# One tile's operands made over three steps, its neighbour's results copied first and summed later, and sums of w_out moved away from the tile switches

## The chip, the cores and the metric

The kernel runs on one core of a Trainium2 chip. The metric is the device time of one execution in microseconds (us), measured on the chip; the profile is one such execution taken by the hardware profiler. The engines are named as in the profile: PE is the matmul engine (PEld its weight loads), DVE the vector engine, ACT the scalar engine, POOL the GpSimd engine, and SP the queue that issues all the DMAs here.

## The reference

The inputs are q, k and v for 8 batches, 8 heads, 576 tokens and 64 elements a head, a weight for the norm, and two weight matrices. Cut to what matters:

```python
kv = np.einsum('bhsd,bhse->bhde', k, v)
out = np.einsum('bhsd,bhde->bhse', q, kv)
rms = np.sqrt(np.mean(out * out, axis=-1, keepdims=True) + 1e-06)
attn = out / rms * g_norm
x = attn.transpose(0, 2, 1, 3).reshape(4608, 512)
h = x @ w_in                          # w_in is 512 x 2048
g = h * (1.0 / (1.0 + np.exp(-h)))
return g @ w_out                      # w_out is 2048 x 512
```

All in float32. The two large products are nearly all of the work.

## The kernel before

**Tiles and steps.** The 4608 tokens are nine tiles `t` of 512 (`TN`), and d_ff is 16 blocks of 128. float32 products are made of three matmuls each: every operand is split into an upper part (a rounded copy, made by ACT) and a lower part (what the rounding lost, a subtraction), and upper times upper, upper times lower and lower times upper are added up in PSUM.

Tiles 0 and 1 use plain products. From tile 2 the product with w_in is made with seven products of half-size blocks in place of eight (Strassen's scheme): `pair_step(t, i)` handles blocks `i` and `i + 8`, eight steps to a tile. Tiles 7 and 8 (`OUT7 = 7`) use seven products for w_out also: `seven_step(t, i)`. In it PE alternates between the w_in products of step `i` (`product(m, i, ...)`, 42 matmuls) and the w_out products of the step before it (`Half.multiply`, 42 matmuls, 21 for each `Half` of the tile's tokens) in four windows. So a seven-step is 84 matmuls of 128x128 by 128x256, and a pair step 90.

All code is written out in the order in which each engine executes it; there is no planner. `first_jobs`, `mid_jobs` and `last_jobs` hold work that is placed by hand at a third of a step `g = 16 t + 2 i` (a pair step or a seven-step spans `g` and `g + 1`).

**What the change touches.**

- The operands of the w_in products. `sums_of_x` makes four sums of the tile's quarters (x_sums, on DVE, 128x512), and `make_operand(m)` makes the upper part of operand `m` on ACT and the lower part on DVE or POOL. Each tile's operands overwrite those of the tile before, so `prepare` makes operand `m` in the last step (`i = 7`) of the tile before, right after the product that read the old one.
- The results of the w_out products. In PSUM each `Half` has seven sums in four banks: banks with (1, 2), (3, 5), (7, 6), and a bank with number 4 of both halves. `Half.results` adds them, from PSUM, to the two output chunks of the half: one copy on ACT and seven adds on DVE of 128x256, then two stores.
- The results of tile 6, the last of a plain w_out product: `project` copies a bank to SBUF after its last matmul, on ACT or DVE by turns, and stores it.
- `make_out_sums(j)`: the combinations of w_out that the last two tiles need, made on POOL over eight thirds of a step, split by ACT and DVE and stored to DRAM. One starts every eight steps from step 48, which is the beginning and the middle of tiles 3 to 6.
- `x_stages`: the scaling of the attention result to x32, a transpose and a multiply on DVE.
- The pool `tmp` has five places. The result copies (`ob`), the sums' tiles `s23` and `s41`, `x_sums`, `yT` and `sq` rotate through it, so that a tile can have to wait for the store of an earlier one.

Of the kernel before, what the change touches and what calls it, by code (L numbers as in the profile page):

```python
# [35 lines left out]
def linear_attention_rms_silu_ffn(  # L36
# [22 lines left out]
    nc = tc.nc  # L59
# [468 lines left out]

    def project(t, f, gh, gl, bank, n, cs):
# [7 lines left out]
        if f == last:  # L537
            ob = tmp.tile([P, S], F32, name="ob", tag="tmp")[:, :cs.stop - cs.start]
            (nc.scalar.copy if n % 2 else nc.vector.tensor_copy)(out=ob, in_=bank)
            nc.sync.dma_start(out=out[t * TN + n * P:t * TN + (n + 1) * P, cs], in_=ob)  # L540
# [8 lines left out]
    operands, x_sums, once = {}, {}, {}  # L549
# [130 lines left out]
    def make_operand(m, engine=nc.vector):  # L680
        j, x, _ = seven[m]
        upper, lower = operand(j)[:, 0], operand(j)[:, 1]
        nc.scalar.copy(out=upper, in_=x())
        engine.tensor_tensor(out=lower, in0=x(), in1=upper.bitcast(F32), op=ALU.subtract)

    def product(m, i, out, start=True, check=True):
        j, _, a_of = seven[m]
        x = operand(j)
        n = 0
        for c in range(2):  # L690
            for a, b in ((0, 1), (1, 0), (0, 0)):
                nc.tensor.matmul(  # L692
                    out=out, lhsT=a_of(i, a, c), rhs=x[:, b, c], start=start and n == 0, stop=n == 5,
# [88 lines left out]
    class Half:  # L782
# [57 lines left out]
        def banks(self, free, last):  # L840

            pairs = ((1, 2), (3, 5), (7, 6))
            self.out, self.opens = {}, {1, 3, 7}
            for (m, n), bank in zip(pairs, free):
                self.out[m], self.out[n] = bank[:, low], bank[:, high]
            self.out[4] = last[:, (low, high)[self.half]]
# [9 lines left out]
        def multiply(self, j, *ms):  # L856
            for m in ms:
                for n, (g, a) in enumerate(((self.hi, 1), (self.hi, 0), (self.lo, 0))):
                    nc.tensor.matmul(  # L859
                        out=self.out[m], lhsT=g[m], rhs=self.weight(m, j, a),  # L860
                        start=j == 0 and n == 0 and m in self.opens, stop=j == HF - 1 and n == 2,
                        skip_group_check=True,
                    )

        def results(self, t):
# [7 lines left out]
            def add(to, x, y, op=ALU.add):  # L873
                nc.vector.tensor_tensor(out=to, in0=x, in1=y, op=op)

            def store(tile_, chunk):
                row = t * TN + self.half * H + chunk * P
                nc.sync.dma_start(out=out[row:row + P, :], in_=tile_)

            return [  # L880
                lambda: nc.scalar.copy(out=p1, in_=out_of[1]),
                lambda: add(second[:, low], out_of[2], p1),
                lambda: add(u2, out_of[6], p1),
                lambda: add(u4, u2, out_of[5], ALU.subtract),
                lambda: add(first[:, low], out_of[3], u4),
                lambda: add(u3, out_of[7], u2),
                lambda: add(first[:, high], u3, out_of[5], ALU.subtract),
                lambda: store(first, 0),
                lambda: add(second[:, high], out_of[4], u3),
                lambda: store(second, 1),  # L890
            ]
# [18 lines left out]
    sevens = []  # L910

    def seven_step(t, i, groups):

        g = t * NF + 2 * i
        fresh, later = i == HF - 1 and t + 1 < NT, i + 1 < HF or t + 1 < NT
        if not sevens:
            once["products"], once["seventh"] = h_bank(), h_bank()
            once["forms"] = block("wi", HF + 5, F32).rearrange("p a n -> p a n")
            sevens.extend(Half(h) for h in range(2))
        before = (t, i) > (OUT7, 0)  # L920
        if (t, i) == (OUT7, 1):
            free = [ps_at.tile([P, 512], F32, name="at", tag=tag) for tag in ("at", "other")] + [once["seventh"]]
            last, *others = [acc_bank() for _ in range(4)]
            sevens[0].banks(free, last)
            sevens[1].banks(others, last)
        first, second = sevens
        j = (i - 1) % HF
        ends = before and i == 0
        scratch = place("scratch", 3, F32)
        p1, u2 = scratch[:, 1, 0], scratch[:, 1, 1]  # L930
# [3 lines left out]

        def old(n):
            for item in groups[:n]:
                project(*item)
            del groups[:n]

        def window(n):  # L940
            if groups:
                old(2)
            elif before:
                which = (first, second)[n // 2]
                which.multiply(j, *(which.order[:4], which.order[4:])[n % 2])
# [5 lines left out]
        def prepare(*ms):  # L951
            for n, m in enumerate(ms if fresh else ()):
# [422 lines left out]
```

## Time and profile before

| | us |
|---|---|
| median of 3 runs | 837.14 |
| lowest and highest | 833.77, 838.43 |
| the profiled execution, own time | 836.62 |
| its span in the trace | 834.7 |
| PE busy | 809.9 (97% of the span) |
| DVE busy | 586.6 (70%) |
| ACT busy | 385.4 (46%) |
| POOL busy | 200.9 (24%) |
| granted PE clock, mean over the span | 0.993 |

The profiled execution's time stands 0.5 us under the median and the span 1.9 us under its own time. A share of busy time is an average over the whole span; where PE is idle is read from its timeline.

### The profile page before, as it was taken

The page shows a single profiled execution, that of the slowest core. Times are in us where ns is not written, and L with a number is a line of the kernel's source. Part 1 is how long each engine was busy: PE and PEld are TensorE (multiplying, and loading weights), DVE is VectorE, ACT ScalarE, POOL GpSimd, SP SyncE. Part 2 cuts the span into 40 slices and gives each one's busy share as a digit, 9 for nine tenths or more (in the row PEclk, how much of TensorE's full clock was granted, in tenths as well). Part 3 has the DMA queues.
Part 4 walks back from the last instruction along what each step waited for, and adds up shares of the span by engine and source line. Part 5 has one row for each costly group of instructions (what it writes and reads, how often), then busy time and mean ns, then how long its engine had stood idle before and what let it go on. Part 6 is the DMA issues. An engine that isn't in the chain of part 4 may idle for free.

```text
span 834.7 us, 18341 instructions
## 1 busy us (share of the span) xinstructions
PE 809.9 (97%) x7388; PEld 800.1 (96%) x7388; DVE 586.6 (70%) x1184; ACT 385.4 (46%) x816; POOL 200.9 (24%) x193
## 2 busy tenths in 40 slices
PE   8999999999999999999999999999999999989996
PEld 7999999999999999999999999999999999888996
DVE  4999948786766666667866687577766667775666
ACT  4787545444542455335533463354434333442442
POOL 2798773331200043003120132004300000010000
PEclk9999999999999999999999999999999999999998
DMA  9993012356434453554527353745333576545552
GB/s 347 412 389 115 1 59 102 152 199 211 166 101 160 160 181 126 183 184 159 202 95 270 119 194 102 258 151 186 111 134 135 190 243 204 179 165 177 180 195 92
DMA packets 59670, 145.89 MB, mean 175 GB/s; under 512 B 5826, under 2 KB 20162, under 8 KB 59586
## 3 DMA queue, kind: packets, MB, share of 16 engines
q1 hardware_dynamic: 59586, 144.73, 50.3%
q8 instruction: 58, 0.95, 0.5%
q14 instruction: 26, 0.21, 0.1%
HBM read 118.49 MB, written 26.21 MB: 173 GB/s over the span
## 4 chain that ended last, share of the span: by engine, by line
PE 82%; DVE 7%; DMA 5%; ACT 2%; POOL 2%; issue 1%; SPq 1%; DVEq 0%; ACTq 0%; POOLq 0%
PE acc L494 32%; PE hp L692 29%; PE hp L494 9%; PE acc L859 4%; DMA wi<-in_moe_w_in 3%; PE at L859 2%; PE at L274 2%; PE hp L859 1%; DMA out<-ob 1%; DVE gl L706 1%; DMA k<-in_k 1%; PE at L307 1%; PE at L308 1%; PE at L309 1%; DVE x L335 1%
## 5 line engine op out<-in xcount | busy, mean ns | idle before, releaser
L494 PE MATMUL acc<-wo,gh 128*128 128x256 f32 x1792 | 279.5, 277 | 0.0
L494 PEld LDWEIGHTS acc<-wo,gh 128*128 128x128 f32 x1792 | 238.7, 188 | 0.4
L692 PE MATMUL hp<-x_second,wi 128*128 128x256 f32 x1344 | 172.5, 280 | 5.0 <-DVE gf L745 4.6
L494 PE MATMUL acc<-wo,gl 128*128 128x256 f32 x896 | 174.5, 276 | 0.0
L692 PEld LDWEIGHTS hp<-x_second,wi 128*128 128x128 f32 x1344 | 161.9, 189 | 7.2 <-DVE gf L745 5.4
L494 PEld LDWEIGHTS acc<-wo,gl 128*128 128x128 f32 x896 | 135.0, 188 | 0.0
L692 PE MATMUL hp<-operand,wi 128*128 128x256 f32 x1008 | 127.5, 278 | 3.3 <-DVE gated L1001 3.3
L692 PEld LDWEIGHTS hp<-operand,wi 128*128 128x128 f32 x1008 | 120.2, 188 | 4.6 <-DVE gated L1001 2.1
L295 POOL TENSOR_TENSOR ql<-q,qh 128x576 fp32r<-128x576 f32 x24 | 36.4, 1515 | 180.9 <-ACT qh L294 172.2
L596 POOL TENSOR_TENSOR s<-wo 128x512 f32<-128x512 f32 x16 | 23.8, 1500 | 156.9 <-DVE x L335 122.5
L744 ACT COPY wi<-hp 128x256 f32<-128x256 f32 x40 | 14.9, 372 | 89.0 <-PE hp L692 89.0
L702 ACT ACTIVATE gh<-gf 128x512 fp32r<-128x512 f32 x40 | 25.3, 633 | 56.5 <-DVE gf L757 52.2
L809 ACT ACTIVATE gated<-gated 128x512 f32<-128x512 f32 x32 | 20.3, 633 | 62.2 <-DVE gated L992 45.1
L494 PE MATMUL hp<-x_second,wi 128*128 128x256 f32 x384 | 46.3, 276 | 0.0
L494 PE MATMUL hp<-x,wi 128*128 128x256 f32 x360 | 44.7, 279 | 0.7 <-POOL x L445 0.7
L494 PEld LDWEIGHTS hp<-x_second,wi 128*128 128x128 f32 x384 | 44.9, 188 | 0.1
L494 PEld LDWEIGHTS hp<-x,wi 128*128 128x128 f32 x360 | 42.6, 188 | 1.2 <-POOL x L445 1.0
L702 ACT ACTIVATE gh<-wi 128x512 fp32r<-128x512 f32 x40 | 25.4, 635 | 38.7 <-DVE wi L757 34.7
L745 DVE TENSOR_TENSOR wi<-hp,wi 128x256 f32<-128x256 f32 x20 | 8.5, 424 | 46.2 <-ACT wi L744 46.2
L335 DVE SCALAR_TENSOR_TENSOR x<-o,gcol,yT 128x128 f32<-128x128 f32 (+7 forms) x52 | 37.9, 728 | 1.9
L745 DVE TENSOR_TENSOR gf<-hp,wi 128x256 f32<-128x256 f32 x20 | 8.5, 423 | 40.5 <-ACT wi L744 40.5
L313 ACT ACTIVATE sq<-at 128x256 f32<-128x256 f32 (+1 forms) x56 | 22.9, 409 | 28.9 <-PE at L309 28.2
(193 smaller groups left out, 1439.8 us busy)
## 6 DMA issues: line engine op xcount, KB each, us to landing
wi<-sums_in_dram SPq DMA_DIRECT2D x112, 512.0 KB, 3.4
s<-out_sums SPq DMA_DIRECT2D x48, 256.0 KB, 4.6
out<-ob SPq DMA_DIRECT2D x36, 256.0 KB, 2.3
wi<-in_moe_w_in SPq DMA_DIRECT2D x16, 512.0 KB, 8.0
wo<-in_moe_w_out SPq DMA_DIRECT2D x16, 512.0 KB, 9.0
sums_in_dram<-sum_parts SPq DMA_DIRECT2D x16, 512.0 KB, 2.6
out_sums<-wi SPq DMA_DIRECT2D x16, 512.0 KB, 2.9
k<-in_k SPq DMA_DIRECT2D x28, 288.0 KB, 5.1
```

Of the source, the lines that this page charges most:

```text
L274: nc.tensor.matmul(out=self.kv[h], lhsT=self.k[rows, c, :], rhs=self.v[rows, c, :], start=(start and r == 0), stop=(stop and r == 4),)
L295: (nc.vector if self.b == 1 else nc.gpsimd).tensor_tensor(out=self.ql, in0=self.q, in1=self.qh.bitcast(F32), op=ALU.subtract)
L313: nc.scalar.activation(out=self.sq[:, self.w], in_=self.ps, func=AF.Square)
L335: nc.vector.scalar_tensor_tensor(out=to, in0=self.o[:, a:e], scalar=gcol, in1=self.yT, op0=ALU.mult, op1=ALU.mult)
L494: nc.tensor.matmul(out=to[:, at:at + 256], lhsT=stationary, rhs=moving[:, at:at + 256], start=start and at == 0, stop=stop and at == n - 256,)
L596: nc.gpsimd.tensor_tensor(out=to, in0=w[:, 0, :], in1=w[:, 1, :], op=ALU.add)
L692: nc.tensor.matmul(out=out, lhsT=a_of(i, a, c), rhs=x[:, b, c], start=start and n == 0, stop=n == 5, skip_group_check=not check,)
L702: nc.scalar.activation(out=gh, in_=x, func=AF.Silu)
L744: nc.scalar.copy(out=p1, in_=u)
L745: nc.vector.tensor_tensor(out=c1[:, low], in0=v, in1=p1, op=ALU.add)
L809: nc.scalar.activation(out=self.gated, in_=self.gated, func=AF.Silu)
L859: nc.tensor.matmul(out=self.out[m], lhsT=g[m], rhs=self.weight(m, j, a), start=j == 0 and n == 0 and m in self.opens, stop=j == HF - 1 and ...
```

## The change

It has five parts.

1. The operands of tile 8 are no longer made in the last step of tile 7. A step has four places between the windows, called "", "I", "II" and "III", and a table `between` says what runs there. `spread_switch` places the four sums at steps 5 and 6 of tile 7 and the operands from step 6 to step 0 of tile 8. So that an operand can be made while the old one is still read, two operands go to free tiles, and the others each to the place of one that has been read already (`ahead`). All lower parts are made on DVE; none on POOL.
2. The results of tile 7 are copied from PSUM by ACT, four banks whole (128x512), and the adds then run on DVE out of SBUF, over steps 0 to 2 of tile 8 (`after_switch`).
3. The 42 w_out matmuls of a step are one queue, of which the windows take 12, 11, 11 and 8 (`W7`), in place of 12, 9, 12 and 9. After the last step the order of the products is another, and `last_results` does one subtraction per half on POOL and stores the second output chunk in two pieces.
4. The copies of tile 6's results are put off to step 1 of tile 7, all four on ACT (`emptied`).
5. `make_out_sums` starts four steps later each time, and the second `x_stages` of the last batch are at steps 1, 4, 6 and 8 after the tile's start in place of 1, 4, 7 and 10.

```diff
-            (nc.scalar.copy if n % 2 else nc.vector.tensor_copy)(out=ob, in_=bank)
...
+        if f == last and t + 1 == OUT7:
+            emptied.append(lambda: empty(t, bank, n, cs, True))
+        elif f == last:
+            empty(t, bank, n, cs, n % 2)
...
+    def make_upper(m, to):
+        nc.scalar.copy(out=to[0], in_=seven[m][1]())
+
+    def make_lower(m, to):
+        nc.vector.tensor_tensor(out=to[1], in0=seven[m][1](), in1=to[0].bitcast(F32), op=ALU.subtract)
...
+        def copies(self, places):
+
+            self.e = places
+            return [
+                lambda n=n, m=m: nc.scalar.copy(out=places[n], in_=self.bank_of[m]) for n, m in enumerate((1, 3, 7))
+            ]
...
+            return [
+                lambda: add(one[:, high], one[:, high], one[:, low]),
+                lambda: add(three[:, high], three[:, high], one[:, low]),
+                lambda: add(three[:, low], three[:, low], three[:, high]),
+                lambda: add(one[:, low], three[:, high], two[:, high], ALU.subtract),
+                lambda: add(two[:, high], three[:, low], two[:, high], ALU.subtract),
+                upper_rows, lower_rows,
+            ]
...
+            nc.scalar.copy(out=p5, in_=out_of[5])
+            add(u4, u2, p5, ALU.subtract, nc.gpsimd)
...
+    W7 = 12, 11, 11, 8
...
+        ahead.update({
+            1: spares, 6: [block6[:, 0], block6[:, 1]], 2: home(1), 7: home(6), 4: home(2), 5: home(7), 3: home(4),
+        })
+        x = sums_of_x()
+        between.update({
+            (5, "I"): x[:1], (5, "II"): x[1:3], (6, "I"): x[3:], (6, "II"): made_ahead(1, 6),
+            (7, "I"): made_ahead(2), (7, "II"): made_ahead(7, 4), (7, "III"): made_ahead(5),
+        })
...
+            (0, "I"): [c[0], *made_ahead(3)], (0, "II"): [c[1], c[2], a[0], a[1]], (0, "III"): a[2:4],
+            (1, ""): [lambda: nc.scalar.copy(out=fourths, in_=once["fourths"])],
+            (1, "I"): [d[0], d[1], *a[4:6]], (1, "II"): [d[2], a[6], b[0], b[1]], (1, "III"): b[2:4],
+            (2, "I"): b[4:6], (2, "II"): b[6:],
...
-        def prepare(*ms):
-            for n, m in enumerate(ms if fresh else ()):
-                make_operand(m, (nc.gpsimd, nc.vector)[n % 2])
...
-        first.multiply(HF - 1, *first.order)
-        run(first.results(t))
-        second.multiply(HF - 1, 1, 2, 6, 5, 3, 7, 4)
-        run(second.results(t))
+        for half, order in ((first, (1, 2, 6, 7, 5, 3, 4)), (second, (4, 1, 2, 6, 7, 5, 3))):
+            for item in half.items(HF - 1, order):
+                half.multiply(*item[1:])
+        for half in sevens:
+            half.last_results(t, once["partial"][:, half.half])
...
-            x_stages(p, b * NF + 1 + p.c * (3 if b >= OUT7 else 1), 1)
+            x_stages(p, b * NF + (1, 4, 6, 8)[p.c] if b >= OUT7 else b * NF + 1 + p.c, 1)
...
-            spread_out(lambda j=j: make_out_sums(j), 3 * (3 * NF + 8 * j), 1, 1, 1, 1, 1, 1, 1, 1)
+            spread_out(lambda j=j: make_out_sums(j), 3 * (3 * NF + 4 + 8 * j), 1, 1, 1, 1, 1, 1, 1, 1)
```

Where the instructions stand in the queues shows more than the diff. DVE, the end of step 6 of tile 7 and the first half of step 7, before: L1001 and L968 take the w_in products out of PSUM (`hp`), L830, L822 and L825 make the forms (`wi13`) of the gated values, L815 and L836 their lower parts (`gl`, `gs`), L646 the sums of x and L684 a lower part of an operand.

```order
L1001 TENSOR_TENSOR gated_8888<-hp_8880,wi15_3139 128x256
L830 TENSOR_TENSOR wi13_8882<-gated_8883,wi13_8882 128x128
L815 TENSOR_TENSOR gl_8885<-gated_8883,gh_8884 128x384
L646 TENSOR_TENSOR t2_9669<-x32_1_2124,t1_9668 128x512
L646 TENSOR_TENSOR t4_9670<-x32_1_2124,t2_9669 128x512
L822 TENSOR_TENSOR wi13_8882<-gated_8888 128x256
L825 TENSOR_TENSOR wi13_8882<-gated_8888,wi13_8882 128x128
L830 TENSOR_TENSOR wi13_8882<-gated_8888,wi13_8882 128x128
L836 TENSOR_TENSOR gl_8887<-wi13_8882,gh_8886 128x512
L968 TENSOR_TENSOR wi15_3139<-hp_8880,wi15_3139 128x256
L684 TENSOR_TENSOR operand6_2987<-t2_9669,operand6_2987 128x512
L815 TENSOR_TENSOR gl_8890<-gated_8888,gh_8889 128x384
```

The same stretch on DVE now; L1116 stands for L1001, L847, L839 and L842 for the forms, L832 and L853 for the lower parts, L1075 for L968, and L701 is the lower part of an operand.

```order
L1116 TENSOR_TENSOR gated_8888<-hp_8880,partial_9492 128x256
L847 TENSOR_TENSOR wi13_8882<-gated_8883,wi13_8882 128x128
L832 TENSOR_TENSOR gl_8885<-gated_8883,gh_8884 128x384
L839 TENSOR_TENSOR wi13_8882<-gated_8888 128x256
L842 TENSOR_TENSOR wi13_8882<-gated_8888,wi13_8882 128x128
L847 TENSOR_TENSOR wi13_8882<-gated_8888,wi13_8882 128x128
L853 TENSOR_TENSOR gl_8887<-wi13_8882,gh_8886 128x512
L1075 TENSOR_TENSOR partial_9492<-hp_8880,partial_9492 128x256
L832 TENSOR_TENSOR gl_8890<-gated_8888,gh_8889 128x384
L853 TENSOR_TENSOR gs_8892<-wi13_8882,gs_8891 128x512
L701 TENSOR_TENSOR operand4_2948<-x32_1_2124,operand4_2948 128x512
L1093 TENSOR_TENSOR partial_9492<-hp_8880,partial_9492 128x256
```

The two sums and the operand's lower part that stood ahead of gl_8887 and gs_8892 are gone from there, and one lower part stands behind gs_8892.

ACT at the start of tile 6, second pair step, before: two copies of tile 5's results, the first cast of the w_out sums (L602), and L744, the copy out of PSUM that the step's chain begins with.

```order
L539 COPY ob_7912<-acc_6614 128x512
L287 CAST kh_7915<-kvm1_91 128x128
L539 COPY ob_7935<-acc_6616 128x512
L602 CAST wi13_4280<-s23_7786 128x512
L744 COPY wi15_3139<-hp_7941 128x256
L313 ACTIVATE sq_7976<-at_7978 128x256
```

The same on ACT now (L533 is the copy, L761 stands for L744):

```order
L533 COPY ob_7905<-acc_6614 128x512
L287 CAST kh_7908<-kvm1_91 128x128
L533 COPY ob_7927<-acc_6616 128x512
L761 COPY wi15_3139<-hp_7930 128x256
L313 ACTIVATE sq_7965<-at_7967 128x256
```

The cast of the sums is gone from between the second copy and the chain's first copy.

DVE in step 0 of tile 8, from the last add that the second products need (L981) to the adds that the third products need (L992, L993), before: seven adds of results (L874), out of PSUM (`at`, `hp`, `acc`), in one run.

```order
L981 TENSOR_TENSOR wi15_3139<-hp_8880,wi15_3139 128x256
L874 TENSOR_TENSOR ob_9917<-at_9022,e1_9914 128x256
L874 TENSOR_TENSOR e1_9914<-hp_8881,e1_9914 128x256
L874 TENSOR_TENSOR e2_9915<-e1_9914,at_9023 128x256
L874 TENSOR_TENSOR ob_9916<-at_9023,e2_9915 128x256
L874 TENSOR_TENSOR e2_9915<-hp_8881,e1_9914 128x256
L874 TENSOR_TENSOR ob_9916<-e2_9915,at_9023 128x256
L874 TENSOR_TENSOR ob_9917<-acc_9024,e2_9915 128x256
L992 TENSOR_TENSOR gated_8883<-hp_8880,wi15_3139 128x256
L993 TENSOR_TENSOR gated_8888<-hp_8880,wi15_3139 128x256
```

Now, with L1093 for L981, L1107 and L1108 for L992 and L993, and L902 for an add of results:

```order
L1093 TENSOR_TENSOR partial_9492<-hp_8880,partial_9492 128x256
L902 TENSOR_TENSOR e_9854<-e_9854 128x256
L902 TENSOR_TENSOR e_9856<-e_9856,e_9854 128x256
L1107 TENSOR_TENSOR gated_8883<-hp_8880,partial_9492 128x256
L1108 TENSOR_TENSOR gated_8888<-hp_8880,partial_9492 128x256
L902 TENSOR_TENSOR e_9856<-e_9856 128x256
L902 TENSOR_TENSOR e_9854<-e_9856,e_9855 128x256
L839 TENSOR_TENSOR wi13_8882<-gated_8883 128x256
```

Two adds stand where seven stood, and two behind the adds that the products need; the others are a step or two later.

More of the change, by code (lines that the diff above doesn't have):

```diff
@@ L854, in weight, with items @@
             return ring(j, m)[:, a]
[L856 to L865, printed above, removed]
+        def items(self, j, ms):
+            return [(self, j, m, n) for m in ms for n in range(3)]
@@ L921, in seven_step @@
         if (t, i) == (OUT7, 1):
[L922 to L925, printed above, removed]
+            first_banks()
         first, second = sevens
[L927 to L930, printed above, removed]
+        if t + 1 < NT and i == 5:
+            spread_switch()
```

187 lines of the change are left out of this document (127 added, 60 removed).

## The prediction

> **What bounds the kernel now.** I read the page first, then the table of waits, then PE's timeline at the two tile switches that the change touches, then DVE and ACT in the same stretches, and last a step without trouble as the measure.
>
> ```profile
> span 834.7 us, 18341 instructions
> PE 809.9 (97%) x7388; PEld 800.1 (96%) x7388; DVE 586.6 (70%) x1184; ACT 385.4 (46%) x816; POOL 200.9 (24%) x193
> PE hp L692 <- DVE gf L745: 4.6, 4, 1.2
> PE at L859 <- DVE gl L836: 4.2, 3, 2.1
> PE hp L692 <- DVE gated L1001: 3.3, 3, 1.6
> PE acc L859 <- DVE ob L874: 0.9, 1, 0.9
> ```
>
> PE is the bound: busy for 97% of the span. So only what makes PE wait, or runs before its first or after its last matmul, can be won. The waits (total, times, longest) name DVE each time: four waits of 1.2 us in the pair steps, and a few in tiles 7 and 8. PE's timeline at the first matmuls of steps shows what they cost:
>
> ```profile
> 649.83 1.52 PE L692 MATMUL hp<-operand,wi 128*128 128x256 f32 x12
> 661.16 1.65 PE L692 MATMUL hp<-operand,wi 128*128 128x256 f32 x12 [0.97 <-DVE gated L1001]
> 722.20 1.64 PE L692 MATMUL hp<-operand,wi 128*128 128x256 f32 x12
> 726.85 0.38 PE L859 MATMUL at<-s,gl 128*128 128x256 f32 x1 [1.77 <-DVE gl L836]
> 737.47 1.65 PE L692 MATMUL hp<-operand,wi 128*128 128x256 f32 x12 [1.57 <-DVE gated L1001]
> 754.05 0.38 PE L859 MATMUL at<-s,gl 128*128 128x256 f32 x1 [2.08 <-DVE gl L836]
> 763.09 1.58 PE L692 MATMUL hp<-operand,wi 128*128 128x256 f32 x12
> 812.10 1.52 PE L692 MATMUL hp<-operand,wi 128*128 128x256 f32 x12
> ```
>
> Steps 2 to 6 of tile 8 lie between 763.09 and 812.10: 49.01 us, 9.80 each. Step 7 of tile 7 and steps 0 and 1 of tile 8 lie between 722.20 and 763.09: 40.89 us, 11.49 more than three of 9.80. Steps 1 to 6 of tile 7 take 61.04, 2.24 more than six of 9.80.
>
> Two more views explain the size of the loss:
>
> ```profile
> 727.80:731.20 3.40, 3.40 (x19) 0.52 0.19 47
> 755.00:758.30 3.30, 3.30 (x19) 0.54 0.82 228
> 724.84 1.41 POOL L684 TENSOR_TENSOR operand<-x,operand 128x512 fp32r<-128x512 f32 x1 [122.90 <-DVE wi L825]
> 725.04 1.75 DVE L836 TENSOR_TENSOR gl<-wi,gh 128x512 fp32r<-128x512 f32 x1
> 785.44 0.68 DVE L836 TENSOR_TENSOR gs<-wi,gs 128x512 fp32r<-128x512 f32 x1
> ```
>
> The first two are stretches of PE (busy, granted clock, DMA share, GB/s): right after the gaps of 1.77 and 2.08 us the granted clock is half for some 3.4 us, so each of these gaps costs about 1.7 more. The gap of 1.57 has no such stretch behind it. The next three show why DVE is late: its subtraction took 1.75 while POOL subtracted beside it, and 0.68 alone.
>
> **The change, part by part.** The measure is a step of tile 8 without trouble, on DVE and PE:
>
> ```profile
> 787.35 0.42 DVE L981 TENSOR_TENSOR wi<-hp,wi 128x256 f32<-128x256 f32 x1 [1.23 <-ACT gated L980]
> 787.83 1.68 PE L692 MATMUL hp<-x_second,wi 128*128 128x256 f32 x12
> 789.55 0.42 DVE L992 TENSOR_TENSOR gated<-hp,wi 128x256 f32<-128x256 f32 x1 [1.77 <-PE hp L692]
> 789.89 0.41 DVE L993 TENSOR_TENSOR gated<-hp,wi 128x256 f32<-128x256 f32 x1
> 790.73 0.43 DVE L822 TENSOR_TENSOR wi<-gated 128x256 f32<-128x256 f32 x1 [0.43 <-ACT gated L809]
> 791.67 0.42 DVE L1001 TENSOR_TENSOR gated<-hp,wi 128x256 f32<-128x256 f32 x1 [0.18 <-PE hp L692]
> 792.53 1.58 PE L692 MATMUL hp<-operand,wi 128*128 128x256 f32 x12
> ```
>
> The brackets are the free places of DVE: 1.23 us before L981 (place "I"), 1.77 before L992 ("II"), 0.43 before L822 ("III") and 0.18 more before L1001.
>
> *A, the switch to tile 8.* What is put there: sums and lower parts of 0.68 each, adds between SBUF tiles of 0.43 each (L822 has that shape). Step 5: 0.68 in I, 1.36 in II. Step 6: 0.68 and 1.36. Step 7: 0.68, 1.36 and 0.68 in III. Step 0: 0.68 in I, 0.86 in II, 0.86 in III. Step 1: 0.86, 1.29, 0.86. Step 2: 0.86, 0.43. Everything in I and II fits. III is too full by 0.25 once and by 0.43 twice, of which the 0.18 takes a part: 0.57 us in all, and L1001 ends at 792.09, 0.4 before PE's next step starts at 792.53, so at most some 0.4 comes through. That no lower part is on POOL costs DVE 4 x 0.68, which is in these sums, and takes the cause of the 1.75 away. ACT gets seven casts, of which none is new, and seven copies of whole banks in place of two of half a bank; it is busy 46% and its copies stand behind the step's own copy. The PE products that read the first overwritten operands have ended by then; what is queued behind a late cast on ACT is the copy L980, and PE waits for that in the end. SP: the stores of the results stand ahead of the next load of sums and wait for adds in I, which delays that load by under 0.5 us of the half step, 4.9 us, that it has. So the 11.49 go except for 0.4: gain 11.1; ends 5 (half of the gaps stay) and 11.5.
>
> The Trainium skill (Perfetto Trace Analysis, section on optimizing Scalar and DVE operations) says that work of a saturated DVE may be offloaded to Scalar or even GPSIMD, though the shared port may spoil it; that speaks against taking four subtractions back to DVE, and with their 2.7 us on the path the sum would be 2.7 smaller. The 1.75 beside 0.68 here decides for the port.
>
> *B, tile 7 before that.* At the start of step 1, PE waited for L1001, which stood behind this on DVE:
>
> ```profile
> 658.68 0.68 DVE L539 COPY ob<-acc 128x512 f32<-128x512 f32 x1
> 659.28 0.70 DVE L327 STREAM_TRANSPOSE yT<-y 128x512 f32<-128x512 f32 x1
> 660.02 0.75 DVE L335 SCALAR_TENSOR_TENSOR x<-o,gcol,yT 128x512 f32<-128x512 f32 x1
> 692.42 0.86 PE L692 MATMUL hp<-operand,wi 128*128 128x256 f32 x5 [0.71 <-DVE gated L1001]
> ```
>
> The copy goes to ACT, a step later; the transpose and multiply stay: 0.6 of the 0.97 is won. At 692.42 PE waited 0.71 for the same pair in the second half of step 3; now it is in the first half, where 1.45 meets a free place of 1.23 and a window that is two matmuls longer. The four copies on ACT fall where ACT waits for PE. Of the 2.24 I take 1.8. B is 2.4; ends 1.2 and 2.9.
>
> *C, the windows.* PE's third products start 0.06 us after L981 ends (787.35 + 0.42, then 787.83): the window of 9 is too short. The chain gives the price, and the pace without waits:
>
> ```profile
> 778.22 1.55 PE hp L692 x12
> 782.83 1.36 PE hp L692 x12
> 603.75 5.44 PE acc L494 x48
> ```
>
> The twelve matmuls behind that wait took 1.55, others 1.36: 0.19 a step. Two more matmuls are 2 x 5.44 / 48 = 0.23 us of cover. Over 15 steps that is 2.9; I take 2.6, since a full place I or III can eat the cover. Ends: 0, and 4.2 if every step ran at 84 x 0.1133 = 9.52.
>
> *D, the starts of tiles 3 to 6.* ACT in tile 6:
>
> ```profile
> 576.00 0.59 ACT L539 COPY ob<-acc 128x512 f32<-128x512 f32 x1 [2.61 <-DMA out<-ob]
> 576.49 0.62 ACT L602 CAST wi<-s 128x512 fp32r<-128x512 f32 x1
> 577.01 0.38 ACT L744 COPY wi<-hp 128x256 f32<-128x256 f32 x1
> 578.22 2.32 PE L692 MATMUL hp<-x_second,wi 128*128 128x256 f32 x18 [1.23 <-DVE gf L745]
> ```
>
> The second copy waits for a store, since two of the five places in `tmp` are with s23 and s41; behind it stand a cast and L744, for which DVE and then PE wait. With the sums four steps later the copy has a place and the cast is gone. What is late next is `sq`, which takes the place of a copy still being stored; it stands behind L744. The sums' casts and subtractions (2 x 0.62 and 2 x 0.68) now also meet the steps that make operands, where the products read what comes out a step later. I take 4.4 of the 4.6; ends 0 and 4.6.
>
> *E, the end.* After the last step:
>
> ```profile
> 824.52 0.69 DVE L836 TENSOR_TENSOR gs<-wi,gs 128x512 fp32r<-128x512 f32 x1 [0.27 <-ACT gs L833]
> 829.77 0.42 DVE L874 TENSOR_TENSOR ob<-acc,e 128x256 f32<-128x256 f32 x1 [0.74 <-DMA out<-ob]
> 830.90 0.42 DVE L874 TENSOR_TENSOR ob<-acc,e 128x256 f32<-128x256 f32 x1
> ```
>
> DVE ends this at 831.32, with 14 adds. Now there are 12, and the tiles that the stores read are not written again: 0.74 and two of 0.42 go, 1.6, less some 0.2 for POOL's subtraction. PE's own wait of 0.9 goes with number 4 first, but DVE ends last. E is 1.4; ends 0.5 and 2.
>
> The sum is 11.1 + 2.4 + 2.6 + 4.4 + 1.4 = 21.9. From the profiled execution's 836.62 that gives 814.7; the median stands 0.5 above it, so 815.2.
>
> **The rivals.** First: D fails, as ACT still stands before a store (sq and ob share five places). Then 815.2 + 4.4 = 819.6. For it: the 2.61 were such a wait. Against: the copy no longer has a store to wait for.
>
> Second: the half clock has another cause than the gaps and stays, 2 x 1.7: 818.6. The two stretches begin where the two longest gaps end and nowhere else, which speaks against it. This is what the Trainium skill would make of it (TensorE: Matmul & The Clock Gate, section on why this matters for your kernels): only idle gaps over about 3 us throttle PE. The trace differs: 1.77 and 2.08 sufficed.
>
> Third: some loaded steps keep a gap. Each costs the gap, up to 2.1, and 1.7 if the clock falls: two to four such steps give 822 to 830.
>
> Fourth, slower: the loaded steps (5 to 7 of tile 7, 0 to 2 of tile 8) each lose what step 7 lost, 737.47 - 722.20 - 9.80 = 5.47. Four of them make 837.1, no gain; from five on it is slower by more than 0.5%. It decides where inserted work exceeds its place by some 1.8 us, and the largest is 1.36 in 1.77. POOL is idle there, so no 1.75 is in sight.
>
> Fifth: the change does little, because the late operands were not the cause but a load was: 830 to 836. The gaps name DVE, not DMA.
>
> **How the numbers follow.** Forecast 0.62, its own range 811 to 819; first rival 0.11, second 0.03, third 0.18, fourth 0.02, fifth 0.04. The range 810 to 826 leaves out the upper half of the third, the fourth and fifth, and a little below. A measurement here tells some 0.5%, 4.2 us, from no change: under 832.95 is faster: 0.95. Within: 0.03. Slower: 0.02.
>
> **What would show it.** In the profile after: no wait of PE on a lower part over 0.5 us at the switch and no half clock there (A); step 1 of tile 7 within 0.5 us of its due start (B); third products within 1.4 us per twelve (C); no wait of PE in the pair steps and none of ACT on a store ahead of its first copy (D); the last add some 4.5 us behind the last lower part (E). The forecast is wrong if the steps around the switch still differ from the others by over 1 us, or if the tile starts wait on something new.

## The result, and the profile after

The changed kernel takes 813.38 us, median of 4 runs (811.61 to 813.58), against 837.78 us for the kernel before beside it: a ratio of 0.971, 95% interval 0.9675 to 0.9748. The forecast was 815.2. The profiled execution took 813.5, its span is 811.7, 23.0 less than the 834.7 of before.

First lines of the page, then the rows on L880 and L709 of the table of PE's waits (total, times, longest):

```profile
span 811.7 us, 18340 instructions
PE 800.1 (99%) x7388; PEld 794.5 (98%) x7388; DVE 585.2 (72%) x1184; ACT 391.2 (48%) x825; POOL 194.5 (24%) x191
```

```profile
PE hp L880 <- DVE gl L853: 0.4, 1, 0.4
PE hp L709 <- DVE gated L1116: 0.4, 1, 0.4
```

The four waits of the pair steps, the waits on the lower part `gl` at the switch and the one on `ob` at the end have gone from the table; two of 0.4 remain, at the start of step 1 of tile 7 and behind the last step. PE's timeline at the places that were shown of before:

```profile
643.77 1.52 PE L709 MATMUL hp<-operand,wi 128*128 128x256 f32 x12
654.51 1.68 PE L709 MATMUL hp<-operand,wi 128*128 128x256 f32 x12 [0.37 <-DVE gated L1116]
713.97 1.58 PE L709 MATMUL hp<-operand,wi 128*128 128x256 f32 x12
723.87 0.87 PE L709 MATMUL hp<-moved,wi 128*128 128x256 f32 x6
743.02 0.84 PE L709 MATMUL hp<-moved,wi 128*128 128x256 f32 x6
```

Step 7 of tile 7 to step 2 of tile 8 is 29.05 us (713.97 to 743.02) where it was 40.89, and no wait stands in it. The two steps of the switch and the granted clock (PE busy, weight loads, DVE, ACT, POOL, then clock, DMA share, GB/s):

```profile
723.90:733.40 9.50, 9.50 (x86) 9.50 (x85) 7.79 (x21) 5.75 (x13) 0.00 (x0) 1.00 0.58 194
733.50:743.00 9.50, 9.50 (x86) 9.50 (x85) 8.20 (x23) 5.86 (x13) 0.00 (x0) 1.00 0.76 245
```

PE does not pause and the clock is 1.00. Both kernels issue 7388 matmuls, so the starts of the n-th matmul can be set side by side. That gives the gain by place, from the two profiles:

| place | gain, us | forecast there |
|---|---|---|
| up to tile 3 (not touched by the change) | 0.3 | 0 |
| starts of tiles 3 to 6 | 5.75 (1.36, 1.39, 1.48, 1.51) | D 4.4 |
| tile 7, steps 0 to 6 (72.37 to 70.20) | 2.2 | B 2.4 + six of C's 15 steps 1.0 = 3.4 |
| step 7 of tile 7 to step 1 of tile 8 (40.89 to 29.05) | 11.8 | A 11.1 + C 0.5 = 11.6 |
| steps 2 to 7 of tile 8 (58.89 to 57.36) | 1.5 | C 1.0 |
| from the end products to the end (12.79 to 11.34) | 1.45 | E 1.4 |
| sum | 23.0 | 21.9 |

The sum fits, with two terms off by over a microsecond in opposite directions: D too small, tile 7 too large. The median came out 1.8 under the forecast: the profiled execution gained 23.1 where 21.9 were forecast, and the half microsecond that the forecast added for the median is not there in the changed kernel, whose profiled execution stands 0.1 above its median. The experiments go for these two, for the cause of A, and for C and E one by one. Times below are medians where four runs are named, else one profiled execution; where the question is a place, the trace decides, since a single step moves less than runs differ. Lines of the experiments' kernels are a few off those of the changed one where code was added, and the diffs are cut to the lines that matter.

### The profile page after: what moved, and what is told of

Read it like the earlier page. It is cut to its first block, busy times and chain, and to the rows that moved or that the text cites. A ratio compares the mean times of both kernels' runs of the same rounds, so it can differ in the third digit from the quotient of the medians.

```text
span 811.7 us, 18340 instructions
## 1 busy us (share of the span) xinstructions
PE 800.1 (99%) x7388; PEld 794.5 (98%) x7388; DVE 585.2 (72%) x1184; ACT 391.2 (48%) x825; POOL 194.5 (24%) x191
## 4 chain that ended last, share of the span: by engine, by line
PE 91%; DMA 4%; POOL 2%; DVE 1%; issue 1%; ACT 0%; SPq 0%; DVEq 0%; POOLq 0%; ACTq 0%
PE acc L494 36%; PE hp L709 33%; PE hp L494 9%; PE acc L880 5%; DMA wi<-in_moe_w_in 3%; PE at L880 3%; PE at L274 2%; PE hp L880 1%; DMA k<-in_k 1%; PE at L307 1%; PE at L308 1%; PE at L309 1%; POOL wo L213 1%; DMA early_wo<-in_q 1%; POOL wi L213 0%
## 5 line engine op out<-in xcount | busy, mean ns | idle before, releaser
L709 PE MATMUL hp<-x_second,wi 128*128 128x256 f32 x1248 | 156.9, 277 | 0.0
L709 PEld LDWEIGHTS hp<-x_second,wi 128*128 128x128 f32 x1248 | 148.8, 188 | 0.0
L709 PE MATMUL hp<-operand,wi 128*128 128x256 f32 x1008 | 126.6, 277 | 0.4 <-DVE gated L1116 0.4
L709 PEld LDWEIGHTS hp<-operand,wi 128*128 128x128 f32 x1008 | 120.1, 188 | 0.6 <-DVE gated L1116 0.6
L761 ACT COPY wi<-hp 128x256 f32<-128x256 f32 x40 | 14.9, 372 | 92.6 <-PE hp L709 92.6
L494 PE MATMUL hp<-x_second,wi 128*128 128x256 f32 x384 | 46.3, 277 | 0.0
L494 PEld LDWEIGHTS hp<-x_second,wi 128*128 128x128 f32 x384 | 44.9, 188 | 0.1
L603 POOL TENSOR_TENSOR s<-wo 128x512 f32<-128x512 f32 x16 | 21.6, 1353 | 93.3 <-DVE x L335 40.8
L335 DVE SCALAR_TENSOR_TENSOR x<-o,gcol,yT 128x128 f32<-128x128 f32 (+7 forms) x52 | 41.2, 792 | 1.9
```

The costliest lines, as they stand in the source:

```text
L335: nc.vector.scalar_tensor_tensor(out=to, in0=self.o[:, a:e], scalar=gcol, in1=self.yT, op0=ALU.mult, op1=ALU.mult)
L494: nc.tensor.matmul(out=to[:, at:at + 256], lhsT=stationary, rhs=moving[:, at:at + 256], start=start and at == 0, stop=stop and at == n - 256,)
L603: nc.gpsimd.tensor_tensor(out=to, in0=w[:, 0, :], in1=w[:, 1, :], op=ALU.add)
L709: nc.tensor.matmul(out=out, lhsT=a_of(i, a, c), rhs=x[b][:, c], start=start and n == 0, stop=n == 5, skip_group_check=not check,)
L761: nc.scalar.copy(out=p1, in_=u)
```

## The experiments

**D alone undone (`sums_back`).**

```diff
-spread_out(lambda j=j: make_out_sums(j), 3 * (3 * NF + 4 + 8 * j), 1, ...)
+spread_out(lambda j=j: make_out_sums(j), 3 * (3 * NF + 8 * j), 1, ...)
```

> The changed kernel with w_out's sums put back to where they were, four half steps earlier (part D undone, all else kept). If D is as the prediction sized it, the four waits of 1.09 to 1.23 us come back and cost what they are listed with, 4.6: 818.0. If a listed wait costs about 0.27 us more than its number (PE's starts in the two traces drift apart by 1.36, 1.39, 1.48 and 1.51 us at these four places), 5.75: 819.1. If those waits had gone for another reason, 813.4.

Measured: 817.0 (four runs, three at 816.95 to 817.03 and one at 822.56), and the starts drift apart by 1.37, 1.39, 1.51 and 1.53 at the four places: 5.80. ACT's timeline at the start of tile 6, PE's timeline there, the row of the table of PE's waits, and last the same copy on ACT in the changed kernel:

```profile
575.97 0.59 ACT L533 COPY ob<-acc 128x512 f32<-128x512 f32 x1 [2.62 <-DMA out<-ob]
576.45 0.62 ACT L609 CAST wi<-s 128x512 fp32r<-128x512 f32 x1
576.97 0.38 ACT L761 COPY wi<-hp 128x256 f32<-128x256 f32 x1
```

```profile
578.19 2.33 PE L709 MATMUL hp<-x_second,wi 128*128 128x256 f32 x18 [1.24 <-DVE gf L762]
```

```profile
PE hp L709 <- DVE gf L762: 4.7, 4, 1.2
```

```profile
569.43 0.59 ACT L533 COPY ob<-acc 128x512 f32<-128x512 f32 x1 [0.58 <-PE acc L494]
570.79 0.37 ACT L761 COPY wi<-hp 128x256 f32<-128x256 f32 x1 [0.77 <-PE hp L709]
```

The mechanism is the predicted one: the copy waits for a store, the cast stands behind it, then L761, DVE and PE. But waits listed with 4.7 cost 5.8. The whole kernel rose by only 3.5 in the trace (815.2 against 811.7), since tile 7 became 2.3 faster: the next two experiments.

**A wait less in tile 7 (`x_zero`).**

```diff
-x_stages(p, b * NF + (1, 4, 6, 8)[p.c] if b >= OUT7 else ..., 1)
+x_stages(p, b * NF + (0, 4, 6, 8)[p.c] if b >= OUT7 else ..., 1)
```

> The changed kernel with the transpose and multiply of the first quarter (L327, L335) one half step earlier, in the first half of step 0 of tile 7, where DVE has a free 1.70 us for their 1.45. The wait of 0.37 us at the start of step 1 goes. If that wait also sets PE's slow pace for the rest of tile 7 (9.89 us a step against 9.56 in tile 8), the steps of tile 7 become 9.56: 0.37 + 0.27 + 7 x 0.33 = 3.0 less, 810.4. If the slow pace comes from what runs beside PE in tile 7, only 0.64 goes: 812.8, with steps of 9.89.

Measured: 810.68 (four runs, 809.96 to 812.04), ratio to before 0.9685, interval 0.9651 to 0.9719; in the trace 3.0 less than the changed kernel once the start, untouched, is taken off (809.1, with the first steps 0.33 later). The wait is gone and steps 1 to 7 of tile 7 are 9.52 to 9.62 long. In the chain, twelve matmuls of tile 7 and of tile 8 in the changed kernel read:

```profile
694.35 1.41 PE hp L709 x12
697.17 1.41 PE hp L709 x12
765.07 1.36 PE hp L709 x12
```

So PE has two paces at a granted clock of 1.00: 1.36 and 1.41 for twelve, 9.5 and 9.89 a step. The changed kernel entered the long one at its wait of 0.37 in step 1 of tile 7 and kept it to the end of the tile: 2 us of what B and C had won. `sums_back` and, below, `gaps` have the same wait and came out of it at the short pace, so the wait does not fix the pace, it redraws it. Of the 3.0 only the wait itself, 0.37 + 0.27, is thus shown to come from the edit; the other 2.3 or so are the pace, which `sums_back` has in tile 7 too, with the wait still there.

**Waits of known length (`gaps`).** In a table by step:

```diff
+IDLE = {(7, 2): 3, (7, 4): 3, (8, 2): 4, (8, 3): 5, (8, 4): 6, (8, 5): 7, (8, 6): 5}
+for _ in range(IDLE.get((t, i), 0)):
+    nc.vector.tensor_tensor(out=u3, in0=u2, in1=u2, op=ALU.add)
 product(3, i, v, False, False)
```

> The changed kernel with useless adds of 0.41 us on DVE ahead of L1116: 3 in steps 2 and 4 of tile 7, 4, 5, 6, 7 and 5 in steps 2 to 6 of tile 8. PE then waits at the next step's start for about 0.42 n - 0.6 us: 0.7, 0.7, 1.1, 1.5, 1.9, 2.3, 1.5, together 9.7. If a listed wait costs itself: 823.2. If it costs 0.27 more: 825.1. On top of it the half clock: if a gap of about half of a 3.41 us window brings it, the gaps of 1.9 and 2.3, perhaps one of 1.5, are followed by 3.4 us at half clock, 1.7 us each: 828 to 830. If only gaps over 3 us do, the clock stays 1.00 throughout. If waits redraw PE's pace, the steps of tile 7 behind the two waits may come out at 9.56 instead of 9.89, some of those of tile 8 at 9.89.

Measured: 826.89 in one run, span 825.1. PE's starts behind the five waits in tile 8, and the granted clock behind the second, third and fourth of them:

```profile
753.55 0.95 PE L709 MATMUL hp<-moved,wi 128*128 128x256 f32 x6 [1.24 <-DVE gated L1119]
765.08 0.97 PE L709 MATMUL hp<-moved,wi 128*128 128x256 f32 x6 [1.71 <-DVE gated L1119]
777.10 1.65 PE L709 MATMUL hp<-moved,wi 128*128 128x256 f32 x6 [2.16 <-DVE gated L1119]
791.02 1.65 PE L709 MATMUL hp<-moved,wi 128*128 128x256 f32 x6 [2.62 <-DVE gated L1119]
803.88 0.97 PE L709 MATMUL hp<-moved,wi 128*128 128x256 f32 x6 [1.71 <-DVE gated L1119]
```

```profile
766.70:770.10 3.40, 3.40 (x32) 3.40 (x31) 2.27 (x6) 1.26 (x3) 0.00 (x0) 1.00 0.26 89
776.90:780.20 3.30, 3.10 (x14) 3.11 (x15) 2.42 (x7) 1.69 (x4) 0.00 (x0) 0.50 0.66 224
790.60:793.90 3.30, 2.88 (x13) 2.88 (x14) 2.65 (x8) 1.55 (x3) 0.00 (x0) 0.50 0.72 215
```

Against the changed kernel PE lost 1.51, 1.99, 3.89, 4.23 and 1.99 us at these waits. The three without half clock cost their number plus 0.27 or 0.28. The other two cost 1.45 and 1.33 more on top, which is the price of the half clock; the prediction had taken 1.7. In tile 7 the wait of 0.79 at 674.05 put what follows it at the long pace (10.0 instead of 9.6 in the next step), the wait of 0.67 at 694.78 ended it. So both theories on waits held, and in this run the half clock begins between 1.71 and 2.16, not near 3. The total stayed under the 828 to 830 that the half-clock theory gave, since a half clock cost 1.4 and most of tile 7 ran at the short pace.

**C alone undone (`old_windows`).** `W7 = 12, 9, 12, 9`.

> The changed kernel with the windows of 12, 9, 12, 9 multiplies again (part C undone). As predicted, each of 15 steps loses 0.17 to 0.19 us before its third products: 2.6 to 2.9, so 816.1. Rival: the short window costs only some 0.05 us a step of waiting, and the rest of the 0.24 us by which the steps of tile 8 now are shorter is PE's slow pace (0.1177 us a matmul instead of 0.1133) that each such small wait sets off for the next 10 to 80 matmuls. Then tile 7, which in the changed kernel runs at the slow pace throughout, loses 0.05 a step or even gains, tile 8 loses 0.24 a step, and the time is 813.5 to 815.5.

Measured: 815.37 (four runs, 814.11 to 816.01), 2.0 above the changed kernel. The profiled execution is the fastest of the four, with a span of 812.3. From step 1 of tile 7 to the end products it is 0.8 longer, not 2.6. In tile 8 each step is 9.73 instead of 9.56, in the chain:

```profile
738.24 1.53 PE hp L709 x12
747.97 1.53 PE hp L709 x12
```

where the changed kernel has 1.36: 0.17 a step, as predicted. In tile 7 steps 1 to 6 are 0.36 shorter together: behind the small wait in steps 2 to 4 PE ran at the short pace for half a step (9.80 for 9.89), in steps 5 and 6 it mostly did not (9.86 and 9.87). So the size per step was right in tile 8, and in tile 7 it was hidden under the pace. The other three runs have no trace, so how much of the 2.0 between the medians is pace is not shown. The rival's reason for tile 8 (that the long pace follows each wait) is not what the trace shows; its small total came out for tile 7.

**A: which part of the operand work cost what.** Six kernels, all with the results as in the changed kernel. `one_step` makes the operands in one step, in the free places I, II, III:

```diff
-(6, "II"): made_ahead(1, 6), (7, "I"): made_ahead(2), (7, "II"): made_ahead(7, 4), (7, "III"): made_ahead(5),
+(7, "I"): made_ahead(1, 6), (7, "II"): made_ahead(2, 7), (7, "III"): made_ahead(4, 5),
```

> The changed kernel with the operands of tile 8 made in the one step that precedes it (step 7 of tile 7: two in place I, two in II, two in III, the seventh in step 0 of tile 8), in the same spare places, subtractions on DVE. The measure is PE's time from the start of step 7 of tile 7 to that of step 2 of tile 8: 29.05 us in the changed kernel, 40.89 before. If POOL's port was the cause of the old loss, DVE alone gets through nearly all: place III is too full by one more subtraction (0.6), of which 0.33 us of slack takes half, so a wait of some 0.3 at step 0 that costs 0.6: 29.6 to 30. If the amount of work in one step was the cause, the old loss of step 7 comes back, 5.5: 34.5. Total: 814 or 819.

`one_step_pool` gives four subtractions to POOL on top:

```diff
+engine = nc.gpsimd if m in ahead and m in (1, 2, 4, 3) else nc.vector
+engine.tensor_tensor(out=to[1], ...)
```

> As one_step, but four of the seven subtractions (numbers 1, 2, 4 and 3) on POOL again. If the port is the cause: POOL's 1.4 us subtractions slow those of DVE beside them from 0.68 to 1.75 and its adds from 0.43 to about 1.3, L1116 and L853 of step 7 come late, and the stretch of 29.05 us becomes 32 to 35, with half clock if a wait passes 1.75. If offloading relieves DVE, which then has only one subtraction in each place: 29.05 to 29.4, below one_step. Total: 817 to 820, or 813.5.

`pool_lowers` is the changed kernel with that line alone:

> The changed kernel, spread over steps as it is, with the subtractions of numbers 1, 2, 4 and 3 on POOL. If the port is the cause, one DVE operation beside each is longer by up to 1.07, in places that have 0.4 to 0.7 us left once a subtraction has gone from them: the stretch is 29.05 to 30.5, waits of PE of up to 0.4. If offloading relieves DVE: 29.05. So here the two differ little; what it shows is whether the spreading alone would have been enough.

Measured, for the stretch of 29.05: `one_step` 29.40 (812.69, four runs), `one_step_pool` 29.56 (812.56, four runs), `pool_lowers` 29.07 (812.75, one run). In these places both theories fell: neither POOL beside DVE nor the amount of work in one step brings the old loss back. That POOL slows DVE is there all the same. POOL's first subtraction and three of DVE's in `one_step_pool` (L702 in both), from the timelines:

```profile
715.53 1.56 POOL L702 TENSOR_TENSOR moved<-x,moved 128x512 fp32r<-128x512 f32 x1 [100.41 <-ACT moved L698]
```

```profile
716.01 1.63 DVE L702 TENSOR_TENSOR wi<-t,wi 128x512 fp32r<-128x512 f32 x1
718.31 1.37 DVE L702 TENSOR_TENSOR operand<-x,operand 128x512 fp32r<-128x512 f32 x1 [0.34 <-ACT operand L698]
720.38 1.00 DVE L702 TENSOR_TENSOR x_second<-t,x_second 128x512 fp32r<-128x512 f32 x1
```

1.63, 1.37 and 1.00 for 0.68, but in places where DVE waits in the changed kernel. So a new theory: what counts is what stands on DVE and ACT ahead of the work that PE needs next. `old_places` moves the same work to where the kernel before had it, into the spare tiles; `own_tiles` keeps the places and writes each operand over its own predecessor. Both keep the four subtractions of `one_step_pool` on POOL:

```diff
 # old_places
+(7, ""): made_ahead(1, 6), (7, "II"): made_ahead(2, 7), (7, "IV"): made_ahead(4, 5), (7, "V"): made_ahead(3),
 # IV: behind first.first_forms(), V: ahead of window(3)
...
-(0, "I"): [c[0], *made_ahead(3)],
+(0, "I"): [c[0]],
```

```diff
 # own_tiles
-1: spares, 6: [block6[:, 0], block6[:, 1]], 2: home(1), 7: home(6), 4: home(2), 5: home(7), 3: home(4),
+m: home(m) for m in (1, 6, 2, 7, 4, 5, 3)
```

> As one_step_pool (which kept the stretch of 29.05 us within 0.7, though POOL slowed DVE's subtractions to 1.63, 1.37 and 1.00), but with the operand work where the kernel before has it in step 7 of tile 7: numbers 1 and 6 ahead of the lower parts of the second half's sums (L853), 4 and 5 behind the first half's, number 3 in step 7 as well. New theory: neither the port nor the amount of work cost the old 5.5 us of step 7, but work that stands on DVE, ACT and POOL ahead of a lower part for which PE comes 1 to 2 us later. Then a wait of 1.5 to 2 us on gl L853 comes back, with half clock if it passes 1.75: stretch 31 to 33, total 814.5 to 817. If it was the tiles (the operands written over their own, after PE's last product with them): 29.1 to 29.8, since here they go to the spare places.

> As one_step_pool, but each operand is made in its own tile, behind PE's last product with the old one. If the place in the order is what counts (new theory): within 0.5 of one_step_pool's stretch, 29.1 to 30. If waiting for PE to release the tile was the cause: casts start later by up to 2 us, L1093 and L1116 stand behind them, 31 to 34.

Measured: `old_places` 32.32 (817.66), `own_tiles` 30.15 (815.69). Against `one_step_pool` the place costs 2.8, the tile 0.6, half of it the long pace in step 1 of tile 8. Another 2.0 of `own_tiles` is that pace to the end of tile 8, 9.89 a step. PE in `old_places`, then three rows of DVE and one of POOL from its timelines:

```profile
727.03 0.95 PE L710 MATMUL hp<-moved,wi 128*128 128x256 f32 x6 [1.80 <-DVE gated L1118]
730.29 0.38 PE L881 MATMUL at<-s,gl 128*128 128x256 f32 x1 [0.34 <-DVE gl L854]
```

```profile
716.25 0.68 DVE L854 TENSOR_TENSOR gl<-wi,gh 128x512 fp32r<-128x512 f32 x1
725.21 1.34 DVE L702 TENSOR_TENSOR x_second<-t,x_second 128x512 fp32r<-128x512 f32 x1 [0.84 <-ACT x_second L698]
726.47 0.41 DVE L1118 TENSOR_TENSOR gated<-hp,partial 128x256 f32<-128x256 f32 x1
717.45 1.29 POOL L702 TENSOR_TENSOR moved<-x,moved 128x512 fp32r<-128x512 f32 x1 [100.65 <-ACT moved L698]
```

I had expected the long wait on `gl` in step 7; it came at the start of step 0, on `gated`. There a lower part of an operand stands ahead of L1118 on DVE; it waits 0.84 for its cast and takes 1.34. The `gl` of step 7 took 0.68 and was done before POOL began. Something still lacked, and on DVE of before the sums of x stand ahead of that lower part. `places_and_x` puts them back too:

```diff
-(5, "I"): x[:1], (5, "II"): x[1:3], (6, "I"): x[3:],
-for t in range(2, OUT7 + 1):
+for t in range(2, NT):
     spread_out(sums_of_x, 3 * (t * NF - 3), 1, 1, 1, 1)
```

> As old_places, and the four sums of x (L653) back at the seam of steps 6 and 7 of tile 7, where the kernel before has them: two of them, 1.41 us on DVE, stand ahead of the adds and the lower part gl L853 of step 7. If what stands ahead of a lower part is the cause, that lower part is ready 1.2 us later, then meets POOL's subtraction and takes 1.75 for 0.68, and PE waits some 1.8 us for it, with half clock behind it as in the kernel before: stretch 32.3 + 1.8 + 0.3 + 1.4 = 35.8, step 7 back at 15 us, total 820 to 821. If the sums of x were harmless: 32.3, total 817.7. What the operands cost in the kernel before, after taking off old_results' part, is 40.9 - 34.2 = 6.7, that is 35.7.

Measured: 34.17 (819.1), step 7 back at 14.00. DVE's, POOL's and PE's timelines in step 7; the lower part, POOL's subtraction and PE's wait are the counterparts of rows that the prediction showed of before:

```profile
714.98 1.41 DVE L653 TENSOR_TENSOR t<-x,t 128x512 f32<-128x512 f32 x2
716.31 0.42 DVE L840 TENSOR_TENSOR wi<-gated 128x256 f32<-128x256 f32 x1
717.29 1.76 DVE L854 TENSOR_TENSOR gl<-wi,gh 128x512 fp32r<-128x512 f32 x1
717.13 1.37 POOL L702 TENSOR_TENSOR moved<-x,moved 128x512 fp32r<-128x512 f32 x1 [100.93 <-ACT moved L698]
```

```profile
719.11 0.38 PE L881 MATMUL at<-s,gl 128*128 128x256 f32 x1 [1.69 <-DVE gl L854]
```

The two sums (1.41) make the adds ahead of the lower part 1.2 later (L840 starts 1.25 behind the end of L833, in `old_places` 0.04), and that pushes it into POOL's subtraction, where it takes 1.76. The wait of before is back; the half clock is not (last section), and that is why it stopped at 819.1 and not at 820. The wait takes both: by these rows the sums make the lower part 1.2 late and POOL makes it 1.08 longer, so without POOL an estimated 0.6 of the 1.69 would be left. No run has the old places with every subtraction on DVE, so how the loss of these places divides between the order and POOL is not shown.

**A: the results (`old_results`).** The adds of before in step 0 (one copy on ACT, seven adds out of PSUM for each half), the operands spread as in the changed kernel:

```diff
+(0, "I"): made_ahead(3),
+(0, "II"): [lambda: first.old_results(t - 1)], (0, "VI"): [lambda: second.old_results(t - 1)],
 # VI: behind window(3)
```

> The changed kernel with the results of tile 7 added up as before: one copy of half a bank on ACT and seven adds on DVE that read PSUM, first half's all in step 0 behind its second window, second half's all at the end of step 0; the operands stay spread. If place accounting holds (seven adds of 0.42 are 2.9 where 1.8 are free, a copy ahead of them, and the next step's adds and lower parts behind the second seven): a wait of about 1 in step 0 and one of 2 or more on gl L853 in step 1, the latter with half clock, 0.27 on each: stretch 29.05 + 5 = 33 to 35.5, total 818 to 820. If the old loss of steps 0 and 1 of tile 8 came from the operands still being made there: 29 to 30.

Measured: 34.22 (817.85). PE's two waits and the clock behind the second:

```profile
731.96 0.97 PE L709 MATMUL hp<-x_second,wi 128*128 128x256 f32 x6 [0.43 <-DVE gated L1123]
738.81 0.38 PE L880 MATMUL at<-s,gl 128*128 128x256 f32 x1 [2.25 <-DVE gl L853]
```

```profile
739.70:743.00 3.30, 3.30 (x18) 3.30 (x17) 0.88 (x2) 0.38 (x1) 0.00 (x0) 0.50 0.77 231
```

5.2 of A is the results, with one stretch of half clock in them. With 5.1 for the operands (34.17 - 29.05), which have none, and the second half clock of before at 1.4, that makes 11.7 of the 11.8, if the parts simply add up.

**E alone undone (`old_end`).** The end of the kernel before: its results, its order of multiplies.

> The changed kernel with the old end: first half's seven, its results, second half's seven with number 4 last, results as before with 14 adds and whole-row stores that reuse tiles. Measure: from the first multiply behind the last step to the end of the span, 11.32 us in the changed kernel, 12.74 before. If E is as predicted (the 0.74 us wait on the store and two adds of 0.42 on DVE's path): 12.6 to 12.8, total 814.8. If only PE's own order or the landing of the last store counts: 11.3 to 11.8.

Measured: 813.84 (four runs). From the end products to the end 13.13 against 11.34. The wait on the store is back (DVE's timeline), as is PE's (table of waits):

```profile
806.99 0.42 DVE L931 TENSOR_TENSOR ob<-acc,e 128x256 f32<-128x256 f32 x1 [0.72 <-DMA out<-ob]
808.11 0.41 DVE L931 TENSOR_TENSOR ob<-acc,e 128x256 f32<-128x256 f32 x1
```

```profile
PE acc L880 <- DVE ob L931: 0.9, 1, 0.9
```

1.8 for the forecast 1.4. Some 0.4 of it is the last store: the span ends 3.7 us behind the last add here, 3.3 in the changed kernel. The medians differ by only 0.5. In this trace half of tile 7 ran at the short pace (steps 1 to 6 in 58.42 instead of 59.47), which takes 1.05 of the 1.8 back: at this size the time of a run tells less than the place in a trace.

## Why the prediction was right, step by step

- **A, right in size, half right in cause.** 11.8 with C's share, 11.6 forecast; no wait on a lower part at the switch, no half clock, as said. The size was read off PE's own timeline as what the three steps took too long, so it did not hang on the cause. Place III held one subtraction without any loss for PE: L1116 ended 0.3 ahead of the next step (723.54 and 723.87), so the 0.4 that I let through did not come. What fell short is the reading of the 1.75: it named POOL alone as its cause. POOL's four subtractions cost 0.2 or less in the free places (`pool_lowers`, `one_step_pool` against `one_step`). The 1.75 needed the sums of x as well, which pushed the lower part into POOL's time; with the work spread and POOL kept (`pool_lowers`, 29.07) the loss is gone, so the spreading was enough, and whether taking POOL out would have been enough is untested. The Trainium skill (Perfetto Trace Analysis, section on optimizing Scalar and DVE operations) says that offloading from a saturated DVE may make sense, even to GPSIMD, but may not help because of a shared read port. Here DVE was busy for 72% of the span, and 29.40 without POOL against 29.56 with it shows no gain and no large loss.
- **B, right where it could be seen.** The wait at step 1 went from 0.97 to 0.37, the 0.6 that was forecast. The rest of tile 7 gained 1.6 in this profile, and 3.5 in `sums_back` (61.04 to 57.54) where the pace was short; the forecast for these six steps was 1.8 with another 1.0 of C. The term had no place for the pace.
- **C, right per step, wrong as a sum.** 0.17 in each step of tile 8, nothing in tile 7: about 0.8 in all in the two traces, against 2.6. The medians put it at 2.0. The step that failed is the multiplication by 15 steps: the price of a wait was taken as the same in every step, and the pace in tile 7 took it away.
- **D, the mechanism right, the size too small.** All four waits went and nothing new came, but they were worth 5.75 and not 4.4, above the end that I had given (4.6). The step that failed is the equation of a listed wait with its cost.
- **E, right**: 1.45 for 1.4. The last add starts 4.9 us behind the start of the last lower part (803.10 and 808.04), some 4.5 forecast.

The errors of D (+1.35) and of tile 7 (-1.2) nearly cancel, which is luck: neither the price of a listed wait nor the pace was in the prediction. The second rival, that the half clock has another cause, fell: its stretches came with the gaps in `gaps` and `old_results` and stayed away from the shorter or divided ones of `places_and_x`.

## What to carry to other kernels

A free place in front of an engine's wait took the extra work at next to no cost here, even with DVE slowed by POOL beside it; the same work ahead of what the bounding engine needs next cost 2.8 us, 4.6 with the sums of x, POOL beside it in both. So read from the trace what each moved instruction stands ahead of, before counting engine time. Price a wait of PE above its listed number (here 0.27 more), and look behind it at the pace and the granted clock. And before a change of 1 us is judged by medians, compare the starts of the same matmul in two traces, place by place, since the pace elsewhere differs from one execution to the next. The version with the first quarter's transpose and multiply half a step earlier (`x_zero`, 810.68 against 813.38) is the fastest of those run, though the intervals of the two ratios overlap.

## What the hardware showed that I had not expected

**A listed wait costs 0.27 more.** A matmul's record is 0.277 long though the next starts 0.113 behind it, and the first one behind a wait is recorded with up to 0.39 (lengths: least, median, most):

```profile
L709 PE MATMUL hp<-operand,wi x288: 276/277/388, 643.8 to 796.8; 128*128 128x256 f32 x144
```

The idle time is counted from the end of the last record: 0.277 - 0.113 = 0.16 is lost before it, and 0.11 in the longer first matmul. That is 0.27, as found at the seven waits of 1.09 to 1.71 that had no half clock behind them: four of before, three of `gaps`.

**Half clock followed windows of which more than half was idle, not a length of gap.** The trace's record of the granted clock changes only on a grid of 3.413 us. With the listed gaps laid on this grid:

| kernel, gap | largest share of one window | half clock behind it |
|---|---|---|
| old_places 1.80 | 36% | no |
| places_and_x 1.91, 1.69 | 41%, 42% | no |
| before 1.57 | 46% | no |
| gaps 1.71, 1.71 | 50%, 50% | no |
| before 1.77 | 52% | yes |
| gaps 2.16 | 57% | yes |
| before 2.08, gaps 2.62 | 61%, 62% | yes |
| old_results 2.25 | 66% | yes |

Each time it lasts one window, the next one. The limit is not sharp, though: after the last matmul of `pool_lowers` and of `one_step_pool` 52% and 56% of a window were idle, and the next window was still at 1.00. So from 57% on half clock followed each time, up to 50% never, and what decides between them stays open. A gap of 1.91 that falls across a border stayed free of half clock while one of 1.77 inside a window did not. The Trainium skill (TensorE: Matmul & The Clock Gate, section on why this matters for your kernels) warns of idle gaps over about 3 us; here 1.77 was enough.

**Two paces at full clock.** 113 and 118 ns a matmul with the granted clock at 1.00, kept over hundreds of matmuls, redrawn by a wait. The wait can be too short to be listed: in `one_step_pool`, `own_tiles` and `old_end` the long pace began behind a single matmul of tile 7 that was followed 0.19 us later in place of 0.113. In the changed kernel the six matmuls of each step of tile 8 whose operand and weights both lie in `wi` tiles start about 119 ns apart, and the long pace ended at the first of these; in `own_tiles`, which has none, it went on through tile 8. What decides between the two paces stays open: the same wait of 0.37 led to both, in the changed kernel and in `gaps`.
